# Attention and feed-forward on one core: weighting k's bits, adding x's small term and adding the divisors' small term on ScalarE in place of VectorE

## The chip, the core and the metric

The kernel runs on one core of a Trainium2 chip. The metric is the device time of one execution in microseconds, the median of the runs shown. Five engines work side by side: TensorE (PE, with its weight loads as PEld), VectorE (DVE), ScalarE (ACT), GpSimd (POOL) and SyncE (SP). Each carries out its own list of instructions in order; semaphores make one wait for another. SP, POOL and ACT also issue DMAs.

## The reference

There are 4 batches of 8 heads, 768 positions and 64 dimensions. Attention is allowed only between positions that fall into the same of 64 hash buckets; the result goes through a feed-forward block.

```python
q_bits = (np.einsum('bhsd,dk->bhsk', q, proj) > 0)      # 6 bits each
k_bits = (np.einsum('bhsd,dk->bhsk', k, proj) > 0)
mask = q_bucket[:, :, :, None] == k_bucket[:, :, None, :]
scores = np.where(mask, scale * q @ k.T, -1e9)
attn = exp(scores - max); attn = attn / (attn.sum(-1) + 1e-09)
x = attn @ v                                             # to (3072, 512)
h = x @ w_in                                             # (3072, 2048)
out = (h * erf(softplus(h))) @ w_out
```

## The kernel before

Attention goes over 16 pairs of heads; a pair fills the 128 partitions. For every pair there is a score stage and an av stage.

In the **score stage**, PE makes 12 blocks of scores (score, L557). A block is two bfloat16 matmuls of the bits and four float32 matmuls of q and k, and fills one of three PSUM slots named "big", which are used in turn. The bits are arranged so that two positions of one bucket add nothing to a score and others add a very large negative number; for that k's bits are multiplied by a weight of 2^100 times a small whole number. ACT takes the exponential of every block (exponential, L584) and so frees its slot: block k+3 needs exponential k.

In the **av stage**, PE multiplies the exponentials by v (weigh, L642; 12 matmuls for each half of the keys and each half of the queries). After it, PE makes the signs' inputs of a later pair (bits_of, L845) and the sums of the exponentials, the divisors, of an earlier pair (divisor, L687). Both write one "big" slot, the one before that of block 0 of the next pair. ACT reads that slot twice: sign_of (L854) writes the bits' signs to the tile sg, and keep_divisor (L698) copies the divisors to z. Block 2 needs the slot, and so both of them.

The small tile sg has q's and k's signs. DVE multiplies k's half by the weight (weigh_bits, L864), and POOL sends sg to DRAM (leave_bits, L874) and places it in the tile of the pair's bits (place_bits, L883), from which the next score stage reads.

ACT copies av's two halves to x (leave, L708). No bucket may divide by zero, so every query gets a tiny attention to all keys: the exponentials of the even half have one column more, of ones, so that av's column HS has the sum of v; DVE multiplies it by EPS = 2^-100 to get ev (leave_plain, L714). The divisor gets S x EPS: z goes to DRAM, comes back as 128x12 (spread, gather, on SP), DVE adds S x EPS and takes the reciprocal (invert, L744 and L747), SP sends it out and reads it back widened to r (ungather, widen), DVE makes (x + ev) x r (normalise, L773), and SP sends x to DRAM (send).

Beside this, DVE sums the exponentials (sum_keys, L630) and converts the weights of the feed-forward block from the halves of 64-bit numbers, with two activations on ACT (square_high, L477, and keep_normal, L484; both write a tile "keep"); POOL fetches them. ACT also squares q and k for a bound (measure, L663, tile "junk").

The order on each engine is set by a planner (arrange): each step has an engine, a cost, a rank and the steps that it comes after; the planner plays the stage through with these costs and emits the steps in the order in which they would start, the lowest rank first among those that could start at once. PE's steps form one chain in a fixed order. For instance:

```python
op(weigh_bits, (i,), "DVE", 0.33, (0, n - 6, 1), (("sign_of", i),))
op(keep_divisor, (i,), "ACT", 0.48, (0, 4 * i + 6, -1),
   (("divisor", i), ("spread", i - 2)))
```

The feed-forward block (from 313 us) has a plan of its own: products with w_in (L1248), a gate made by ACT and DVE, products with w_out (L1361). Its first steps also hold the last pair's divisor, invert and normalise.

Of the kernel before, what the change touches and what calls it, by code (L numbers as in the profile page):

```python
# [54 lines left out]
F32 = mybir.dt.float32  # L55
# [3 lines left out]
AF = mybir.ActivationFunctionType  # L59
ALU = mybir.AluOpType  # L60
# [3 lines left out]
P = 128  # L64
# [4 lines left out]
EPS = 2.0**-100  # L69
# [127 lines left out]
def kernel(  # L197
# [11 lines left out]
    nc = tc.nc  # L209
    B, H, S, D = v.shape  # L210
# [5 lines left out]
    HS = S // 2  # L216
# [9 lines left out]
    scale = 1.0 / D**0.5  # L226
    assert D == 64 and S == 768 and DM == JP * P and NT == B * S and NK == 4

    const = ctx.enter_context(tc.tile_pool(name="const", bufs=1))
    dram = ctx.enter_context(tc.tile_pool(name="dram", bufs=2, space=bass.MemoryType.DRAM))  # L230
    misc = ctx.enter_context(tc.tile_pool(name="misc", bufs=1, space=PSUM))
    small = ctx.enter_context(tc.tile_pool(name="small", bufs=3))
# [7 lines left out]
    ones = const.tile([P, D], F32, name="ones")  # L240
    sgn = const.tile([P, 1], F32, name="sgn")
    tiny2 = const.tile([P, 1], F32, name="tiny2")
    cq = const.tile([P, len(GATE_S) + 1], F32, name="cq")
    w_in_sb = const.tile([P, NK, DFF], F32, name="w_in_sb")
    w_out_sb = const.tile([P, NF, DM], F32, name="w_out_sb")
# [51 lines left out]
    nc.vector.tensor_copy(out=weight_q[D + QR : P, :], in_=weight_q[D : D + QR, :])  # L297
    nc.vector.memset(sgn, -(2.0**-27))
    nc.vector.memset(tiny2, TINY * TINY)
    for j, c in enumerate([b for _, b, _ in GATE_S] + [GATE_BIAS]):  # L300
        nc.vector.memset(cq[:, j : j + 1], c)

# [117 lines left out]
    def attention():  # L420
        NS = NPAIR * 4
        with (
# [15 lines left out]
            junk = ep.tile([P, HS], BF16, name="junk")  # L438
            NE = 2 * GC
            e_even = ep.tile([P, NE, 2, HS + 1], F32, name="e_even")  # L440
            nc.vector.memset(e_even[:, :, :, HS : HS + 1], 1.0)
            e_odd = area[:, 0 : NE * S].rearrange("p (n a c) -> p n a c", n=NE, a=2)
            e_last = {}
            pairs = {}
# [250 lines left out]
            def keep_divisor(i):  # L695
                d = pairs[i]
                d["z"] = home(i, "z")
                nc.scalar.copy(out=d["z"], in_=d.pop("z_ps"))  # L698

            def leave(h):  # L700

                i, half = divmod(h, 2)
                d = pairs[i]
                cols = slice(half * HS, (half + 1) * HS)
                if half == 0:
                    d["x"] = home(i, "x")
                x = d["x"][half] if i == NPAIR - 1 else d["x"][:, cols]
                nc.scalar.copy(out=x, in_=d["av", half][:, 0:HS])  # L708

            def leave_plain(i):  # L710

                d = pairs[i]
                d["ev"] = small.tile([P, 1], F32, name="ev", tag="ev")
                nc.vector.tensor_scalar(  # L714
                    out=d["ev"],
                    in0=d["av", 0][:, HS : HS + 1],
                    scalar1=EPS,
                    scalar2=None,
                    op0=ALU.mult,
                )  # L720

            def spread(i):
# [17 lines left out]

            def invert(i):
                d = pairs[i]
                zc = d["zc"]
                nc.vector.tensor_scalar(  # L744
                    out=zc, in0=zc, scalar1=S * EPS, scalar2=None, op0=ALU.add
                )
                nc.vector.reciprocal(out=zc, in_=zc)  # L747

            def ungather(i):
                d = pairs[i]  # L750
# [16 lines left out]
            def normalise(i):  # L767
                d = pairs[i]
                parts = ((d["x"], d["r"]),)
                if i == NPAIR - 1:  # L770
                    parts = ((d["x"][n], d["r"][:, n * HS : (n + 1) * HS]) for n in range(2))
                for x, r in parts:
                    nc.vector.scalar_tensor_tensor(  # L773
                        out=x, in0=x, scalar=d["ev"][:, 0:1], in1=r, op0=ALU.add, op1=ALU.mult
                    )

            def send(i):
                b, j = divmod(i, JP)
# [45 lines left out]
            def op(fn, args, engine, cost, rank, after=(), **more):  # L824
                name = (fn.__name__,) + args
                ops.append(Op(name, engine, cost, rank, lambda: fn(*args), after=after, **more))
# [34 lines left out]

            def weigh_bits(i):

                nc.vector.tensor_scalar(  # L864
                    out=sg[D:P, :],
                    in0=sg[D:P, :],
                    scalar1=weight_q[D:P, 0:1],
                    scalar2=None,
                    op0=ALU.mult,
                )  # L870

            def leave_bits(i):
# [47 lines left out]
            for what, n in order:  # L920
                free = slots[-3] if len(slots) >= 3 else ()
                if what == "score":
                    i = n // 4
                    after = (("double_first",) if i == 1 else ("place_bits", i),)
                    for c in range(GC):
                        free = slots[-3] if len(slots) >= 3 else ()
                        pe(score, (n, c), 0.82 if n or c == 2 else 0.17, after + free)
                        slots.append((("exponential", n, c),))
                elif what == "bits":
                    pe(bits_of, (n,), 0.80 if n > 1 else 1.44, (("start_pair", n),) + free)  # L930
                    slots.append((("sign_of", n),) if n > 1 else (("place_first",),))
                elif what == "divisor":
                    if n != NPAIR - 3:
                        free = ()
                        slots[-1] += (("keep_divisor", n),)
                    else:
                        slots.append((("keep_divisor", n),))
                    pe(divisor, (n,), 0.72, (("sum_keys", n, last_sum(n)),) + free)
                else:
                    h = n // 2  # L940
                    after = (("exponential", n, GC - 1),)
                    if n % 2 == 0:
                        after += (("leave", h - 2), ("leave_plain", (h - 2) // 2))
                    pe(weigh, (n,), 2.0, after)
            sums_after = {}
            for i in range(NPAIR):
# [25 lines left out]
            for i in range(NPAIR - 1):  # L972
                op(
                    keep_divisor,
                    (i,),
                    "ACT",
                    0.48,
                    (0, 4 * i + 6, -1),
                    (("divisor", i), ("spread", i - 2)),
                )  # L980
            for h in range(NH):
                i = h // 2
                op(leave, (h,), "ACT", 0.48, (0, 2 * h, -2), (("weigh", 2 * h + 1), ("send", i - 3)))
                if h % 2 == 0:
                    op(leave_plain, (i,), "DVE", 0.15, (0, 2 * h, 0), (("weigh", 2 * h + 1),))
            for i in range(NPAIR):
                n = 4 * i
                if i:
                    op(
                        start_pair,  # L990
                        (i,),
                        "SP",
                        3.6,
                        (0, n - 6),
                        (("weigh", n - 9), ("bits_of", i - 1))
                        + tuple(("measure", i - 3, m, half) for m in range(2) for half in range(2)),
                        late=3.5,
                    )
                    if i == 1:
                        op(place_first, (), "ACT", 0.9, (0, n - 2, 9), (("bits_of", i),))  # L1000
                        for ab in (1, 0):
                            op(weigh_first, (ab,), "DVE", 0.43, (0, n - 2, 1), (("place_first",),))
                        op(double_first, (), "DVE", 0.35, (0, n - 2, 2), (("weigh_first", 0), ("weigh_first", 1)))
                    else:
                        op(sign_of, (i,), "ACT", 0.6, (0, n - 6, 9), (("bits_of", i), ("leave_bits", i - 1)))
                        op(weigh_bits, (i,), "DVE", 0.33, (0, n - 6, 1), (("sign_of", i),))
                        op(leave_bits, (i,), "POOL", 0.7, (0, n - 6, 2), (("weigh_bits", i),), late=4.0, far=True)
                        op(
                            place_bits,
                            (i,),  # L1010
                            "POOL",
                            1.2,
                            (0, n - 6, 3),
                            (("leave_bits", i), ("score", n - 5, 2), ("clean", i - 2)),
                            late=3.6,
                        )
# [11 lines left out]
                    continue  # L1028
                op(spread, (i,), "SP", 0.4, (0, n, 0), (("keep_divisor", i),), late=3.5, far=True)
                op(gather, (i,), "SP", 0.35, (0, n, 1), (("spread", i),), late=4.5, far=True)  # L1030
                op(invert, (i,), "DVE", 0.4, (0, n + 8, 3), (("gather", i),))
                op(ungather, (i,), "SP", 0.35, (0, n, 2), (("invert", i),), late=3.0, far=True)
                op(
                    widen,
# [4 lines left out]
                    (("ungather", i), ("normalise", i - 2)),  # L1039
                    late=5.0,  # L1040
                )
                op(normalise, (i,), "DVE", 1.02, (0, n + 8, 4), (("widen", i), ("leave", 2 * i + 1)))
                op(send, (i,), "SP", 0.35, (0, n, 4), (("normalise", i),), late=2.2)
            for n in range(2):
                op(clean, (n,), "POOL", 1.4, (0, 4 * n), (("score", 4 * n + 3, 2),), late=0.3)
# [787 lines left out]
```

## Time and profile before

| what | value |
|---|---|
| runs shown | 904.62, 904.65, 905.37 us; median 904.65 |
| the profiled execution | 904.72 us, its span 902.9 us |
| granted TensorE clock | 0.998 |
| attention | from the start to 313 us |
| PE busy in 20 to 320 us | all of it, but for 0.02 us |
| DVE busy in 145 to 170 us | 23.78 of 25 us |
| ACT busy in 145 to 170 us | 21.23 of 25 us |
| first exponential of a pair (143.49 us) | 0.82 us |
| one activation of measure, and the next start after it | 0.52 us, 0.51 us |

The profile is one execution taken by the hardware profiler. A row of a group gives line, engine, operation, the tiles written and read, shapes and count, then the busy time in us and the mean of one in ns, then the engine's idle time ahead of them and what ended it. In a timeline, instructions of one kind that follow each other are merged; the second number is the length of the merged row. An engine's neighbouring instructions overlap a little, so the distance of two starts can be less than the first one's length. The ends of matmuls are modelled, so a short wait of PE need not be seen as idle time; it is seen in the distance of starts.

### The profile page before, as it was taken

What the parts mean: (1) busy time and instruction counts of PE and PEld (TensorE: products, weight loads), DVE (VectorE), ACT (ScalarE), POOL (GpSimd) and SP (SyncE); (2) the same over time, 40 slices, a digit from 0 to 9 for tenths busy, and PEclk for the clock granted to TensorE, in tenths of its full rate; (3) what the DMA queues carried; (4) which work ended last, traced back from release to release, by engine and by line L of the source; (5) the groups of instructions that cost most, each with busy time, mean ns of one, the idle gap of its engine ahead of it and who ended that gap; (6) DMA issues with size and microseconds to landing.
All of it is one profiled execution on the core that took longest, in us unless ns stands there. A gap on an engine that the chain in (4) does not pass through costs nothing.

```text
span 902.9 us, 12780 instructions
## 1 busy us (share of the span) xinstructions
PE 894.3 (99%) x5016; PEld 670.9 (74%) x5016; DVE 668.5 (74%) x837; ACT 563.3 (62%) x808; POOL 57.9 (6%) x95
## 2 busy tenths in 40 slices
PE   9999999999999999999999999999999999999997
PEld 5455554455544588888888888888888888888886
DVE  5999999999999879995666556666776666655652
ACT  6788888788886668855645455545655555545520
POOL 1211211111110000000000001000100010000000
PEclk9999999999999999999999999999999999999999
DMA  9547655667551322202231013211421122111211
GB/s 228 149 128 183 200 166 142 196 173 195 154 157 60 101 89 65 82 36 70 59 106 58 14 49 103 82 36 47 105 83 36 36 74 78 35 36 57 63 68 50
DMA packets 65156, 86.82 MB, mean 96 GB/s; under 512 B 34364, under 2 KB 47772, under 8 KB 65088
## 3 DMA queue, kind: packets, MB, share of 16 engines
q1 hardware_dynamic: 56528, 63.81, 24.8%
q0 software_dynamic: 8112, 21.66, 8.6%
q8 instruction: 41, 0.67, 0.3%
q10 hardware_dynamic: 448, 0.46, 0.2%
q14 instruction: 27, 0.22, 0.1%
HBM read 64.67 MB, written 17.30 MB: 91 GB/s over the span
## 4 chain that ended last, share of the span: by engine, by line
PE 99%; DVE 0%; issue 0%; ACT 0%; DVEq 0%
PE M L1361 32%; PE X L1248 29%; PE st L557 17%; PE av L642 14%; PE M L1248 3%; PE bits L845 1%; PE bits L687 1%; PE warm L807 0%; PE bits L377 0%; PE z_ps L687 0%; DVE e L1288 0%; DVE h L1270 0%; ACT both L390 0%; DVE u L1396 0%; DVE norms L1754 0%
## 5 line engine op out<-in xcount | busy, mean ns | idle before, releaser
L1288 DVE SCALAR_TENSOR_TENSOR e<-w,e 128x1024 f32<-128x1024 f32 x144 | 173.7, 1220 | 8.4 <-ACT w L1282 3.9
L1248 PE MATMUL X<-area,w_in_sb 128*128 128x256 f32 x680 | 160.6, 379 | 0.0
L1282 ACT ACTIVATE w<-h,cq 128x1024 f32<-128x1024 f32 x144 | 155.6, 1136 | 0.1
L557 PE MATMUL st<-q,k 64*128 64x384 f32 x768 | 155.1, 482 | 0.0
L1270 DVE TENSOR_TENSOR h<-X,h 128x512 f32<-128x512 f32 x65 | 44.8, 689 | 144.4 <-PE X L1248 144.4
L1248 PEld LDWEIGHTS X<-area,w_in_sb 128*128 128x128 f32 x680 | 129.2, 190 | 17.6
L1361 PE MATMUL M<-w_out_sb,h 128*128 128x256 f32 x576 | 141.1, 379 | 0.0
L1248 PE MATMUL X<-area 128*128 128x256 f32 x520 | 122.8, 379 | 0.0
L1361 PEld LDWEIGHTS M<-w_out_sb,h 128*128 128x128 f32 x576 | 109.4, 190 | 14.9
L1266 ACT COPY h<-X 128x512 f32<-128x512 f32 x85 | 49.3, 580 | 111.4 <-PE X L1248 111.3
L1248 PEld LDWEIGHTS X<-area 128*128 128x128 f32 x520 | 98.8, 190 | 13.4
L1278 ACT ACTIVATE e<-h,cq 128x1024 f32<-128x1024 f32 x48 | 55.1, 1148 | 85.9 <-DVE h L1270 85.8
L1361 PE MATMUL M<-wt,S 128*128 128x256 f32 x384 | 95.1, 379 | 0.0
L557 PEld LDWEIGHTS st<-q,k 64*128 64x128 f32 x768 | 68.8, 187 | 29.7 <-issue 27.2
L630 DVE TENSOR_TENSOR area<-area 128x1536 f32<-128x1536 f32 (+1 forms) x46 | 79.2, 1723 | 7.5 <-ACT area L584 6.3
L1361 PEld LDWEIGHTS M<-wt,S 128*128 128x128 f32 x384 | 73.0, 190 | 9.9
L584 ACT ACTIVATE e_even<-st 128x768 f32<-128x768 f32 x96 | 70.6, 822 | 0.4 <-PE st L557 0.3
L584 ACT ACTIVATE area<-st 128x768 f32<-128x768 f32 x90 | 68.0, 817 | 0.0
L642 PE MATMUL av<-e_even,v 128*64 128x385 f32 x384 | 65.6, 490 | 0.0
L557 PE MATMUL st<-both 64*128 64x384 bf16 x384 | 63.5, 323 | 0.3 <-ACT both L390 0.3
L1303 DVE TENSOR_TENSOR h<-h,e 128x1024 f32<-128x1024 f32 x48 | 57.9, 1220 | 4.6 <-ACT e L1299 4.6
L642 PE MATMUL av<-area,v 128*64 128x384 f32 x360 | 60.6, 486 | 0.0
(129 smaller groups left out, 976.8 us busy)
## 6 DMA issues: line engine op xcount, KB each, us to landing
wt<-wt SPq DMA_DIRECT2D x24, 768.0 KB, 4.2
raw<-in_w_out_dram POOLq DMA_DIRECT2D x16, 512.0 KB, 4.2
raw<-in_w_in_dram POOLq DMA_DIRECT2D x14, 512.0 KB, 4.6
v<-in_v_dram SPq DMA_DIRECT2D x32, 192.0 KB, 4.6
q<-in_qkT_dram SPq DMA_DIRECT2D x30, 192.0 KB, 4.2
k<-in_qkT_dram SPq DMA_DIRECT2D x30, 192.0 KB, 4.7
r<-rd SPq DMA_DIRECT2D x30, 192.0 KB, 3.7
xs<-x SPq DMA_DIRECT2D x15, 384.0 KB, 3.0
```

Source lines behind the costliest of these rows:

```text
L557: nc.tensor.matmul(out=st[:, ab, 0:HS], lhsT=d["k" + src][rows, keys], rhs=d["q" + src][rows, cols], start=(part == 0), stop=(part == 1),)
L584: nc.scalar.activation(out=e[:, :, 0:HS], in_=st[:, :, 0:HS], func=AF.Exp, scale=scale)
L630: nc.vector.tensor_tensor(out=into, in0=one, in1=two, op=ALU.add)
L642: nc.tensor.matmul(out=d["av", half][rows, 0:w], lhsT=d["v"][:, g * GC + c, rows], rhs=e[:, ab, 0:w], start=(g == 0 and c == 0), stop=(g = ...
L1248: nc.tensor.matmul(out=d[where][:, u, :], lhsT=a[:, kc, f : f + P], rhs=b[:, kc, :], start=(first and u == 0 and kc == 0), stop=(last and ...
L1266: nc.scalar.copy(out=quarter(p, q), in_=st[p][where])
L1270: nc.vector.tensor_tensor(out=h, in0=st[p][where], in1=h, op=ALU.add)
L1278: nc.scalar.activation(out=s, in_=unit(p, v), func=AF.Sigmoid, bias=cq[:, n : n + 1])
L1282: nc.scalar.activation(out=q, in_=unit(p, v), func=AF.Sigmoid, scale=GATE_S[j][0], bias=cq[:, j : j + 1])
L1288: nc.vector.scalar_tensor_tensor(out=s, in0=st[p].pop(("q", v, j)), scalar=GATE_S[j][2], in1=s, op0=ALU.add, op1=ALU.mult,)
L1303: nc.vector.tensor_tensor(out=h, in0=h, in1=st[p].pop(("s", v)), op=ALU.mult)
L1361: nc.tensor.matmul(out=banks[name][:, sub, :], lhsT=a[:, u, sub * P : (sub + 1) * P], rhs=b[:, u, :], start=(c == 0 and k == 0), stop=(c = ...
```

## The change

Three small computations go from DVE to ACT, each into an activation with a per-partition operand where that can be.

- k's weight: the DVE multiply becomes an activation Copy whose scale is the weight's column (64x384, in place in sg).
- ev: the extra column holds EPS in place of ones, so av's column HS is ev itself; ACT copies it (128x1), and both copies of av to x become activations Identity with ev as the bias. normalise is a plain multiply by r.
- the divisors' S x EPS: the copy of z becomes an activation Identity with a column "least" as the bias; invert is the reciprocal alone.

The planner's costs and ranks are changed to match, and so the order that it emits.

```diff
+    least = const.tile([P, 1], F32, name="least")
...
+    nc.vector.memset(least, S * EPS)
...
-            nc.vector.memset(e_even[:, :, :, HS : HS + 1], 1.0)
+            nc.vector.memset(e_even[:, :, :, HS : HS + 1], EPS)
...
                 d["z"] = home(i, "z")
-                nc.scalar.copy(out=d["z"], in_=d.pop("z_ps"))
+                nc.scalar.activation(
+                    out=d["z"], in_=d.pop("z_ps"), func=AF.Identity, bias=least[:, 0:1]
+                )
...
-                nc.scalar.copy(out=x, in_=d["av", half][:, 0:HS])
-
-            def leave_plain(i):
-
-                d = pairs[i]
-                d["ev"] = small.tile([P, 1], F32, name="ev", tag="ev")
-                nc.vector.tensor_scalar(
-                    out=d["ev"],
-                    in0=d["av", 0][:, HS : HS + 1],
-                    scalar1=EPS,
-                    scalar2=None,
-                    op0=ALU.mult,
+                if half == 0:
+                    d["ev"] = small.tile([P, 1], F32, name="ev", tag="ev")
+                    nc.scalar.copy(out=d["ev"], in_=d["av", 0][:, HS : HS + 1])
+                nc.scalar.activation(
+                    out=x, in_=d["av", half][:, 0:HS], func=AF.Identity, bias=d["ev"][:, 0:1]
                 )
...
-                zc = d["zc"]
-                nc.vector.tensor_scalar(
-                    out=zc, in0=zc, scalar1=S * EPS, scalar2=None, op0=ALU.add
-                )
-                nc.vector.reciprocal(out=zc, in_=zc)
+                nc.vector.reciprocal(out=d["zc"], in_=d["zc"])
...
-                    nc.vector.scalar_tensor_tensor(
-                        out=x, in0=x, scalar=d["ev"][:, 0:1], in1=r, op0=ALU.add, op1=ALU.mult
-                    )
+                    nc.vector.tensor_tensor(out=x, in0=x, in1=r, op=ALU.mult)
...
-                nc.vector.tensor_scalar(
-                    out=sg[D:P, :],
-                    in0=sg[D:P, :],
-                    scalar1=weight_q[D:P, 0:1],
-                    scalar2=None,
-                    op0=ALU.mult,
+                nc.scalar.activation(
+                    out=sg[D:P, :], in_=sg[D:P, :], func=AF.Copy, scale=weight_q[D:P, 0:1]
                 )
...
-                        after += (("leave", h - 2), ("leave_plain", (h - 2) // 2))
+                        after += (("leave", h - 2),)
...
                     keep_divisor,
                     (i,),
                     "ACT",
-                    0.48,
+                    0.58,
...
-                op(leave, (h,), "ACT", 0.48, (0, 2 * h, -2), (("weigh", 2 * h + 1), ("send", i - 3)))
-                if h % 2 == 0:
-                    op(leave_plain, (i,), "DVE", 0.15, (0, 2 * h, 0), (("weigh", 2 * h + 1),))
+                op(leave, (h,), "ACT", 0.58 if h % 2 else 0.78, (0, 2 * h, -2), (("weigh", 2 * h + 1), ("send", i - 3)))
...
-                        op(weigh_bits, (i,), "DVE", 0.33, (0, n - 6, 1), (("sign_of", i),))
+                        op(weigh_bits, (i,), "ACT", 0.5, (0, n - 6, 10), (("sign_of", i),))
...
-                op(invert, (i,), "DVE", 0.4, (0, n + 8, 3), (("gather", i),))
+                op(invert, (i,), "DVE", 0.23, (0, n + 8, 3), (("gather", i),))
...
-                op(normalise, (i,), "DVE", 1.02, (0, n + 8, 4), (("widen", i), ("leave", 2 * i + 1)))
+                op(normalise, (i,), "DVE", 0.93, (0, n + 8, 4), (("widen", i), ("leave", 2 * i + 1)))
```

## The prediction, as it was put on record

> **What bounds the kernel now.** I read the page's busy times first, then who TensorE (PE) waited for, then the groups of instructions by form over the first 440 us, then the timelines of ScalarE (ACT) and PE beside each other. The page:
>
> ```profile
> PE 894.3 (99%) x5016; PEld 670.9 (74%) x5016; DVE 668.5 (74%) x837; ACT 563.3 (62%) x808; POOL 57.9 (6%) x95
> ```
>
> PE is busy in 99% of the span, and the chain that ended last is PE for 99% of it. A microsecond counts only if PE's stream is held or let go. All of PE's recorded waits are these:
>
> ```profile
> PE warm L807 <- DVE ones L253: 1.0, 1, 1.0
> PE M L1248 <- DVE h L1270: 0.7, 1, 0.7
> PE st L557 <- ACT both L390: 0.3, 1, 0.3
> ```
>
> So VectorE (DVE), though 24 of 25 us busy in most stretches of attention, holds PE in one place only, 0.7 us at 338.22 us, after attention. But this view hides small holds, because the modelled end of a matmul fills them. They show in the chain in order of time, as the distance from one pair's score stage to the next: 19.13 us in most pairs, but 19.42 from 103.93, 19.30 from 180.79 and 19.17 three times: 0.58 us lost in all. What a held pair looks like on ACT, then on PE (start us, length us, engine, line, tiles):
>
> ```profile
> 104.00 0.58 ACT L854 ACTIVATE sg<-bits,sgn 128x384 bf16<-128x384 f32 x1 [0.98 <-PE bits L687]
> 104.48 0.67 ACT L477 ACTIVATE keep<-raw 128x512 f32<-128x512 f32 x1
> 105.03 0.48 ACT L698 COPY z<-bits 128x384 f32<-128x384 f32 x1
> 105.39 2.24 ACT L584 ACTIVATE e_even<-st 128x768 f32<-128x768 f32 x3
> 107.48 0.76 ACT L484 ACTIVATE keep<-keep,tiny 128x512 int32<-128x512 f32 x1
> 108.09 2.25 ACT L584 ACTIVATE e_even<-st 128x768 f32<-128x768 f32 x3
> ```
>
> ```profile
> 104.68 0.33 PE L557 MATMUL st<-both 64*128 64x384 bf16 x2
> 104.84 0.81 PE L557 MATMUL st<-q,k 64*128 64x384 f32 x4
> 105.57 0.34 PE L557 MATMUL st<-both 64*128 64x384 bf16 x2
> ...
> 108.15 0.82 PE L557 MATMUL st<-q,k 64*128 64x384 f32 x4
> 108.99 0.34 PE L557 MATMUL st<-both 64*128 64x384 bf16 x2
> ```
>
> A score block costs PE 0.807 us. Block 2 was due at 105.49 and began at 105.57, 0.05 us after z's end (105.03 + 0.48): the three PSUM slots make block 2 wait for the sign and for z, which read the slot before block 0. In the same way block k+3 waits for exponential k: block 6 began at 108.99, just after the exponential that stood behind the keep (108.09 + 0.84), 0.18 late. That is the place where this change can act: **the first microseconds of each score stage on ACT**.
>
> **The skill.** "ScalarE: Activation LUTs", section "What ACT_TABLE_LOAD costs", says that every per-partition pointer operand (bias or scale) adds about 93 ns to an activation, and that neighbours overlap by about 93 ns. The trace agrees: sign, with a bias pointer, 581 ns beside 472 to 480 for copies of the same size, and z starts 0.48 after sign. Its section "Rules for kernel authors" gives plain adds and multiplies to VectorE; the rows below bear that out here (320 ns on DVE). The forecast takes the trace's durations.
>
> ```profile
> L484 ACT ACTIVATE keep<-keep,tiny 128x512 int32<-128x512 f32 x32 | 23.2, 724 | 0.7
> L773 DVE SCALAR_TENSOR_TENSOR x<-x,ev,r 128x768 f32<-128x768 f32 x15 | 15.1, 1011 | 0.0
> L708 ACT COPY x<-av 128x384 f32<-128x384 f32 x30 | 14.4, 480 | 41.7 <-PE av L642 41.1 <-DVE ev L714 0.5
> L854 ACT ACTIVATE sg<-bits,sgn 128x384 bf16<-128x384 f32 x14 | 8.1, 581 | 11.8 <-PE bits L687 11.5 <-PE bits L845 0.3
> L698 ACT COPY z<-bits 128x384 f32<-128x384 f32 x13 | 6.1, 472 | 0.0
> L864 DVE TENSOR_SCALAR sg<-sg,weight_q 64x384 bf16<-64x384 bf16 x14 | 4.5, 320 | 0.6
> L744 DVE TENSOR_SCALAR zc<-zc 128x12 f32<-128x12 f32 x16 | 2.6, 162 | 0.0
> L714 DVE TENSOR_SCALAR ev<-av 128x1 f32<-128x1 f32 x16 | 2.4, 149 | 0.5 <-ACT x_last L708 0.3 <-ACT x L708 0.2
> ```
>
> **The change part by part.** PE's instruction order is the same in both built programs; DVE's, ACT's, and in a few places POOL's and SP's, are re-planned.
>
> *DVE loses* 16 x 0.149 (ev) + 14 x 0.320 (weigh) + 16 x 0.162 (divisor's add) = 9.5 us, and normalise falls from 1.01 to about 0.96 (the 128x768 sum rows, 958 ns), 0.8 us more. On the path: nothing, since no PE wait in attention ends on DVE. The hold at 338.22 stays: before it DVE idles 0.88 us for PE's bound matmul, so the 0.16 us saved ahead of that only lengthens the idling. The new memset (least) falls into DVE's 3.2 us wait for proj_in at the start.
>
> *ACT gains in the av stage:* one ev copy (128x1; between 0.20, the accumulator read of that size, and 0.48, a whole L708 copy; I take 0.2), 0.03 for the x that waits for it, and 0.1 on each of two x by the pointer rule: 0.43 us a pair. Cover: ACT idles there 0.66, 2.04 and 0.98 us (before the two x and the sign, 156 to 162 us). If it were gone, sign and block 2 would be late. Cost 0. av's PSUM is written again only in the next pair.
>
> *ACT gains at the head of the score stage:* weigh, and z grown by 0.1 to 0.58. Weigh (64x384, from SBUF, scale pointer) has no row. Nearest: L484, pointer, 512 wide, 724 ns; less 128 x 0.83 ns (a 768-wide sign, 0.90, against the 384-wide, 0.58) gives 0.62; sign itself 0.58; below, the Square of this size without a pointer, 0.52. I take 0.60, next start 0.50 later. It waits for sign's write: L484 starts 0.03 after L477's end.
>
> Time from block 0: sign starts at 0.14, ends 0.72; blocks 2, 3, 5 and 6 are due at 1.62, 2.43, 4.05 and 4.86. Before, z ended at 1.09 and the first exponential at 1.85, both with over 0.4 to spare. The new instruction list has two orders:
>
> - Sign, weigh, z (5 pairs). Weigh 0.75 to 1.35, z 1.25 to 1.83, block 2 at 1.88: **0.26 late**. Exponentials start at 1.73 and 2.42 (0.69 apart when ACT is behind); in 4 pairs the plan puts one squaring (measure, 0.51) next, so the third starts at 3.62, ends 4.45, and block 5, now due at 1.88 + 3 x 0.807 = 4.30, begins at 4.50: 0.20 late. In the fifth the measure comes one later: exponential 3 starts at 4.31, ends 5.15; block 6, due at 5.11, begins at 5.20: 0.09. Sum 4 x 0.46 + 0.35 = 2.2 us.
> - Sign, z, weigh (8 pairs). z ends at 1.20, in time. Weigh 1.09 to 1.69, first exponential 1.59 to 2.43, block 3 at 2.48: 0.05 late. A pair of the old trace with a keep in that place (exponential 1.60 after block 0) lost 0.04 in its period; I take 0.04: 0.3 us. Later exponentials regain 0.12 each, so measures or keeps put after the sixth or later cost nothing.
> - One pair has no z: the exponential starts at 1.24, free.
>
> Sum 2.5 us, less the 0.58 of old holds (all in pairs that get the new order) = 1.9; about 0.01 more per held pair (period against counted holds: 0.29 against 0.28), 0.1. **Net +2.0 us.** It is against the profiled execution, 904.72 (span 902.9), which lies 0.07 from the median 904.65: 906.7.
>
> *Queues.* Behind weigh stand the exponentials, as costed. POOL's store of the bits leaves 0.4 to 0.8 us later, with the weight fetch queued behind it; the bits are placed at 147.64 for use at 161.59, the fetch (144.39) is read at 154.31: covered. SP's spread leaves up to 0.8 later; from its issue at 143.57 the gather was issued at 147.30, and the reciprocal came at 155.43, so with a second landing as long over 4 us are spare. The few swaps among SP's and POOL's DMAs fall inside such margins: 0.
>
> **Rivals.**
> 1. *The holds are smaller.* With weigh at its lower end, 0.52, z in the first order starts 0.08 earlier, the first hold is 0.17, and the second order has none: 4 x 0.37 + 0.26 = 1.7, less 0.58 = +1.1: 905.8, which is no change within 0.2%. It decides from weigh under about 0.57. For it: the Square row. Against it: the pointer's 0.1 in sign.
> 2. *DVE's relief is what counts*, ACT absorbing its additions: the 0.58 us of holds and the 0.7 at 338.22 go: 903.4 at best, no measurable gain. For it: DVE at 24 of 25 us. Against it: both large holds stand after ACT's z and exponential, not after DVE.
> 3. *ACT falls behind for good.* If weigh or its wait costs 0.2 us more, the second order holds block 3 by 0.25 (8 x 0.2 = 1.6 more) and the first by 5 x 0.2 = 1.0 more: +4.6, 909.3. For it: scale pointers and chained waits have few rows. Against it: L484's 0.03.
>
> **How the numbers follow.** Forecast 0.53 (906.2 to 908.0), rival 1 0.31, rival 2 0.04, rival 3 0.12. A measurement of this kernel tells about 0.2% (1.8 us) from no change, so the forecast lies just outside that bound, and I leave a tenth of its cases within it: slower 0.60, same 0.38, faster 0.02. The range takes in rival 1's value and part of rival 3's: 905.3 to 908.4.
>
> **What would show it.** PE's score-to-score periods near 19.6 in the five pairs with weigh ahead of z, near 19.17 in the eight others; z ending about 1.83 after block 0 in the five; weigh near 0.60; the stretch from 345 us on unchanged in length; DVE busy about 10 us less, ACT about 17 more. I am wrong if weigh is much shorter, if PE's block 2 doesn't wait for z, or if a hold appears in the av stage.

## The result, and the profile after

The changed kernel takes **910.73 us** (median of 909.55 to 911.01), the kernel before 904.85 beside it: a ratio of 1.0064, interval 1.0054 to 1.0074. It is slower, as forecast, but by 5.9 us in place of 2.0, and outside the range. Its profiled execution is 910.92 us, with a span of 908.8.

The page's busy times moved between the engines as forecast: DVE has 9.3 us less, ACT 17.4 more, and PE, whose work is the same, 3.6 more.

```profile
PE 897.9 (99%) x5016; PEld 672.7 (74%) x5016; DVE 659.2 (73%) x792; ACT 580.7 (64%) x838; POOL 58.1 (6%) x95
```

All of PE's recorded waits, as shown for the kernel before:

```profile
PE st L559 <- ACT z L700: 1.1, 5, 0.2
PE warm L798 <- DVE ones L254: 1.0, 1, 1.0
PE M L1233 <- DVE h L1255: 0.7, 1, 0.7
PE st L559 <- ACT both L392: 0.3, 1, 0.3
```

The first row is new: block 2 waits for z in five pairs, 0.2 us each. The 0.7 us that PE waits after attention stayed. Nothing else appears, though more than this was lost; again the small holds are hidden by the modelled ends of matmuls.

The lengths of the new instructions were forecast well. ACT's groups by form, over the first 440 us (busy us, mean ns):

```profile
L855 ACT ACTIVATE sg<-sg,weight_q 64x384 bf16<-64x384 bf16 x14 | 8.5, 610 | 0.4
L845 ACT ACTIVATE sg<-bits,sgn 128x384 bf16<-128x384 f32 x14 | 8.1, 580 | 8.0 <-PE bits L689 7.8 <-PE bits L836 0.2
L700 ACT ACTIVATE z<-bits,least 128x384 f32<-128x384 f32 x13 | 7.5, 576 | 0.1
```

Weigh takes 0.61 us (forecast 0.60), z 0.58 (0.58). So the lengths don't explain the miss.

**Where the time went.** From block 1 of the first pair's score stage to block 1 of the last pair's the kernel before takes 288.18 us, the changed one 293.26: **+5.08**. I call this stretch "attention" below. From there to the end, 606.3 became 606.5. The stretch began 0.62 later (at 9.02 for 8.40 us); in the profiled runs of all kernels below it begins anywhere from 8.08 to 9.18, with the change and without, so this is not counted as the change's. The last 0.3 us of the profiled difference lie outside the span.

The distance from one pair's score stage to the next was 19.13 in most pairs before. Now it is 19.72 in four of the five pairs with weigh ahead of z and 19.61 in the fifth (forecast near 19.6); 19.42 to 19.43 in four of the eight pairs with z ahead of weigh and 19.52 to 19.53 in the other four (forecast 19.17); 19.25 in the pair without z (forecast 19.13). A pair with z ahead of weigh, on ACT (start us, length us, engine, line, tiles):

```profile
67.06 0.58 ACT L845 ACTIVATE sg<-bits,sgn 128x384 bf16<-128x384 f32 x1 [0.87 <-PE bits L689]
67.54 0.57 ACT L700 ACTIVATE z<-bits,least 128x384 f32<-128x384 f32 x1
68.14 0.61 ACT L855 ACTIVATE sg<-sg,weight_q 64x384 bf16<-64x384 bf16 x1
68.77 4.33 ACT L586 ACTIVATE e_even<-st 128x768 f32<-128x768 f32 x6
73.08 0.81 ACT L586 ACTIVATE area<-st 128x768 f32<-128x768 f32 x1
73.91 0.72 ACT L486 ACTIVATE keep<-keep,tiny 128x512 int32<-128x512 f32 x1
```

Read the starts against the ends. z starts 0.10 before sign's end, as neighbours do in this trace where neither needs the other's result. (Where one does, it starts 0.03 after the other's end, as the prediction took for weigh behind sign.) Weigh starts at 68.14, 0.025 us **after** z's end (68.11), and the first exponential 0.024 **after** weigh's end (68.75). Then six exponentials take 4.33 us, 0.72 for each, overlapped again; but the first activation of another kind, the keep at 73.91, again starts 0.025 after the end of the one before. Each of these three places costs about 0.12. On PE in the same pair:

```profile
67.74 0.33 PE L559 MATMUL st<-both 64*128 64x384 bf16 x2
...
68.55 0.33 PE L559 MATMUL st<-both 64*128 64x384 bf16 x2
...
69.64 0.34 PE L559 MATMUL st<-both 64*128 64x384 bf16 x2
```

Blocks start 0.81 apart, but block 3, due at 69.36, starts at 69.64, after the first exponential: 0.28 late. A pair with weigh ahead of z, on ACT, then on PE (blocks 1 and 2):

```profile
47.34 0.58 ACT L845 ACTIVATE sg<-bits,sgn 128x384 bf16<-128x384 f32 x1 [0.87 <-PE bits L689]
47.96 0.61 ACT L855 ACTIVATE sg<-sg,weight_q 64x384 bf16<-64x384 bf16 x1
48.59 0.58 ACT L700 ACTIVATE z<-bits,least 128x384 f32<-128x384 f32 x1
49.07 1.50 ACT L586 ACTIVATE e_even<-st 128x768 f32<-128x768 f32 x2
```

```profile
48.03 0.33 PE L559 MATMUL st<-both 64*128 64x384 bf16 x2
...
49.22 0.34 PE L559 MATMUL st<-both 64*128 64x384 bf16 x2 [0.23 <-ACT z L700]
```

z starts 0.025 after weigh's end, not 0.10 before it. Block 0 of this pair began at 47.21; z's end, 49.17, lies 1.96 after it, where 1.83 was forecast, and block 2 is 0.39 late in place of 0.26. So the question for the experiments was not how long weigh is but **why it doesn't overlap its neighbours**: because of its function, its pointer, its type, its writing in place, its number of partitions, or the order it stands in.

### The profile page after: what moved, and what is told of

Its sections match the earlier page's. It is cut to its first block, busy times and chain, and to the rows that moved or that the text cites. A ratio compares the mean times of both kernels' runs of the same rounds, so it can differ in the third digit from the quotient of the medians.

```text
span 908.8 us, 12773 instructions
## 1 busy us (share of the span) xinstructions
PE 897.9 (99%) x5016; PEld 672.7 (74%) x5016; DVE 659.2 (73%) x792; ACT 580.7 (64%) x838; POOL 58.1 (6%) x95
## 4 chain that ended last, share of the span: by engine, by line
PE 95%; ACT 3%; DVE 0%; issue 0%; DVEq 0%
PE M L1346 32%; PE X L1233 29%; PE st L559 14%; PE av L644 14%; PE M L1233 3%; PE bits L836 1%; PE bits L689 1%; ACT sg L845 1%; ACT sg L855 1%; ACT z L700 1%; ACT e_even L586 1%; PE warm L798 0%; PE bits L379 0%; PE z_ps L689 0%; DVE e L1273 0%
```

## The experiments

"Ratio" is to the kernel before on the same chip; where there is none, the kernel had one execution, and the reading rests on its trace.

**Is it weigh, or one of the other two moves?** Everything of the change, but weigh back on VectorE with its old cost and rank:

```diff
-                nc.scalar.activation(
-                    out=sg[D:P, :], in_=sg[D:P, :], func=AF.Copy, scale=weight_q[D:P, 0:1]
+                nc.vector.tensor_scalar(
+                    out=sg[D:P, :], in0=sg[D:P, :], scalar1=weight_q[D:P, 0:1], ...
...
-    op(weigh_bits, (i,), "ACT", 0.5, (0, n - 6, 10), (("sign_of", i),))
+    op(weigh_bits, (i,), "DVE", 0.33, (0, n - 6, 1), (("sign_of", i),))
```

> The change with weigh_bits back on VectorE (its old cost and rank); ev, the biased copies of x and the biased z stay on ScalarE. Theory (the weigh instruction alone makes the time, by the holds at the head of each score stage): about the time before, 904.9 +- 0.6, score-to-score periods 19.13 to 19.45 as before, no hold of block 3. Rival (the longer z and the ev and x copies matter too, or the re-planned order does): 906 to 908, with holds left in most pairs.

Measured: 904.84 us, ratio 1.0004 (0.9995 to 1.0013); attention 288.27. The moves of x's and the divisors' small terms are not told from no change. As far as the time can tell, weigh is the whole cost.

The other half: the kernel before with weigh alone on ScalarE (the same instruction and plan entry; z a plain copy).

> The kernel before with weigh_bits alone put on ScalarE (the change's cost and rank); z stays a plain copy, ev and the divisor's add stay on VectorE. Theory: most of the 5.9 us, 908.8 to 910.0, periods of about 19.6 where weigh stands ahead of z and about 19.4 where it stands after it. Rival (it takes the biased z too): under 907.

Measured: 912.07 us, ratio 1.0084 (1.0067 to 1.0101); attention 295.20, +7.0. Weigh alone costs more than the whole change: with other costs around it the plan puts weigh ahead of z in seven pairs, with a squaring right after the first exponential, and these last 19.87 to 19.94 us. The size was missed; what one instruction costs hangs on what the planner sets behind it. One of the seven pairs on ACT, from z on; weigh ended at 48.24:

```profile
48.26 0.48 ACT L698 COPY z<-bits 128x384 f32<-128x384 f32 x1
48.63 0.82 ACT L584 ACTIVATE e_even<-st 128x768 f32<-128x768 f32 x1
49.48 0.52 ACT L663 ACTIVATE junk<-q 128x384 bf16<-128x384 f32 x1
```

The exponential overlaps z by 0.10, but the squaring starts 0.024 after the exponential's end (0.023 to 0.026 in all seven). In the change, where z is an activation with a bias, the squaring behind "weigh, z, exponentials" overlaps by 0.12 or more in all five pairs. So part of the higher price is one stop more in each of these pairs.

**The instruction, or the order that the planner makes of it?** The change's own order on every engine, with only the weigh instruction emitted on VectorE (its planned place kept):

> The change with its plan kept (weigh_bits is still planned on ScalarE at a cost of 0.5, so all instructions are emitted in the change's order), but the weigh instruction itself goes to VectorE. Theory (the instruction on ScalarE makes the holds): none of block 2 and 3, periods 19.13 to 19.25, 904.9. Rival (the change's plan, with squarings right after the second exponential, costs by itself): some holds of block 5 or later stay, 906 to 907.

Measured: 904.19 us, ratio 0.9999 (0.9990 to 1.0007); attention 287.61, all pairs 19.13. The order is innocent; the instruction on ACT is the cost.

The other way, z ahead of weigh in all pairs:

```diff
-    op(weigh_bits, (i,), "ACT", 0.5, (0, n - 6, 10), (("sign_of", i),))
+    op(weigh_bits, (i,), "ACT", 0.5, (0, n - 6, 10), (("sign_of", i), ("keep_divisor", i - 3)))
```

> The change with one more dependency in the plan: weigh_bits comes after keep_divisor of the same slot, so that the order is sign, z, weigh in all pairs. Theory (ahead of z, weigh holds block 2 by 0.39 us and block 5 by 0.19; after z it holds block 3 by 0.28): the five pairs fall from 19.6-19.7 to about 19.4, 1.2 us less than the change, 909.5. Rival (ScalarE's total work sets it, the order moves the hold only): no different from the change, 910.7.

Measured: 910.00 us, ratio 1.0060 (1.0043 to 1.0076); attention 293.59, no shorter than the change's: the rival's answer. In four of the five pairs block 2 is in time now, but block 3 is 0.28 late, and a squaring, planned after the fourth exponential, makes block 7 another 0.22 late: they last 19.64 for 19.72. The fifth got a keep between sign and z, and lasts 20.03 (block 2 is 0.22 late, block 3 another 0.66); one of the eight got the squaring too, and lasts 19.64 for 19.43. The holds were pushed to other blocks.

**Its function?** Weigh as Identity instead of Copy, the pointer kept:

```diff
-                    out=sg[D:P, :], in_=sg[D:P, :], func=AF.Copy, scale=weight_q[D:P, 0:1]
+                    out=sg[D:P, :], in_=sg[D:P, :], func=AF.Identity, scale=weight_q[D:P, 0:1]
```

> The change with weigh as an Identity activation in place of a Copy, with the same scale pointer; the plan is the same. In the change the instruction after weigh starts 0.025 us after weigh's end, where other neighbours overlap by 0.10. If the function Copy is what keeps them apart, they overlap again here, and the holds shrink by about 0.1 (the order weigh, z) to 0.25 (the order z, weigh), some 2 us in all: about 908.5. If the scale pointer, the bfloat16 input or the half of the partitions does it, nothing moves: 910.7.

Measured: 910.55 us; attention 293.29; the gaps are still +0.024 to +0.026. Not the function.

**Its pointer?** A constant scale of 2.0 (the bits' weights are left out):

```diff
-                    out=sg[D:P, :], in_=sg[D:P, :], func=AF.Copy, scale=weight_q[D:P, 0:1]
+                    out=sg[D:P, :], in_=sg[D:P, :], func=AF.Copy, scale=2.0
```

> The change with a constant scale (2.0) in weigh in place of the pointer to the weight's column: the weights of the bits are left out. Plan, shape, bfloat16 and half of the partitions as in the change. If the scale pointer keeps weigh apart from its neighbours, they overlap again by about 0.10, weigh takes about 0.51, and the holds fall to about 0.1 (weigh, z: block 2) and 0 (z, weigh: block 3), the time to about 906. If bfloat16 or the half of the partitions does it, the gaps of 0.025 stay: about 910.

Measured: 908.12 us; attention 292.07. ACT in a pair with z ahead:

```profile
66.45 0.57 ACT L700 ACTIVATE z<-bits,least 128x384 f32<-128x384 f32 x1
67.05 0.52 ACT L855 ACTIVATE sg<-sg 64x384 bf16<-64x384 bf16 x1
67.60 0.81 ACT L586 ACTIVATE e_even<-st 128x768 f32<-128x768 f32 x1
```

Weigh is 0.09 shorter, and still stands alone: it starts 0.025 after z's end (67.02), and the exponential 0.024 after its end. So the pointer costs its 0.09 us, 1.2 us of attention in all, but not the overlap. (The rest of the shorter time lies outside attention: the stretch begins 0.9 earlier, at 8.08, and what follows it takes 605.8.) From the other side, the kernel before with a pointer of ones as the scale in square_high, on all partitions:

```diff
-                nc.scalar.activation(out=sq, in_=high.bitcast(F32), func=AF.Square)
+                nc.scalar.activation(out=sq, in_=high.bitcast(F32), func=AF.Square, scale=ones[:, 0:1])
```

> The kernel before with a scale pointer (a column of ones) in square_high, a float32 activation of all 128 partitions, 32 in all; weigh is on VectorE. If a scale pointer keeps an activation apart from its neighbours, square_high now starts 0.025 after its predecessor's end, its successor likewise, and it takes 0.1 longer; the two pairs with a square between sign and z are held some 0.3 us more, and the time is 905.3 to 906. If the pointer isn't the cause, it overlaps its neighbours by 0.1 as before: 904.8.

Measured: 904.93 us; attention 288.51. The squares grow from 688 to 780 ns, and still overlap by about 0.10 those neighbours that don't need their result.

**Its type?** The kernel before with measure reading bfloat16 zeros (the norms' bound is left out):

```diff
-                    in_=pairs[i]["qk"[n]][:, cols],
+                    in_=junk,
```

> The kernel before with the squarings of measure reading the bfloat16 tile junk (zeros, all 128 partitions) in place of q and k; the bound on the norms is left out. If a bfloat16 input is what keeps an activation apart, measure now starts 0.025 after the exponential ahead of it has ended, and the exponential after it 0.025 after its end, where both overlapped by 0.1 before; the time is 905.5 to 908, as measures stand among the exponentials. If not, it overlaps as before: 904.8.

Measured: 906.12 us, with a late begin (9.18); attention 288.21, as before. The overlaps stay at 0.10 to 0.15. Not the type; and as junk is here both read and written, not the writing in place.

**Its partitions?** Weigh works on the 64 partitions of k's bits. The change with weigh over all 128, q's rows weighted by 1:

```diff
+    nc.vector.memset(weight_q[0:D, :], 1.0)
...
-                    out=sg[D:P, :], in_=sg[D:P, :], func=AF.Copy, scale=weight_q[D:P, 0:1]
+                    out=sg, in_=sg, func=AF.Copy, scale=weight_q[:, 0:1]
```

> The change with weigh over all 128 partitions (q's half with weights of 1), still bfloat16 and in place. If the half of the partitions keeps weigh apart from its neighbours, they overlap by 0.10 now and the time falls to about 907; if the bfloat16 input (or the in-place write) does it, gaps of 0.025 and holds stay as in the change: 910 to 911.

Measured: 906.01 us (905.62 for one execution of the kernel before beside it); attention 289.97, +1.79. The pair shown first for the change (lines are one higher here):

```profile
66.37 0.58 ACT L846 ACTIVATE sg<-bits,sgn 128x384 bf16<-128x384 f32 x1 [0.87 <-PE bits L690]
66.85 0.57 ACT L701 ACTIVATE z<-bits,least 128x384 f32<-128x384 f32 x1
67.31 0.62 ACT L856 ACTIVATE sg<-sg,weight_q 128x384 bf16<-128x384 bf16 x1
67.82 2.91 ACT L587 ACTIVATE e_even<-st 128x768 f32<-128x768 f32 x4
```

Twice the rows, the same length (0.616 us), and now weigh starts 0.11 before z's end and the exponential 0.11 before weigh's. The holds of the blocks are nearly those that the prediction gave for the change: 0.26 and 0.19 in the four pairs, 0.26 and 0.08 in the fifth, and by the periods 0.02 to 0.03 in the eight; and the later holds of 0.10 are gone.

And the reverse: the kernel before with measure on the upper 64 partitions (half of the norms left out), nothing else changed:

```diff
+            nc.vector.memset(stats, 0.0)
...
-                    out=junk,
-                    in_=pairs[i]["qk"[n]][:, cols],
+                    out=junk[D:P, :],
+                    in_=pairs[i]["qk"[n]][D:P, cols],
...
-                    accum_out=stats[:, n, i, half : half + 1],
+                    accum_out=stats[D:P, n, i, half : half + 1],
```

> The kernel before with the squarings of measure over partitions 64 to 127 alone, float32 (the norms of each pair's first head are left out). If an activation on half of the partitions is kept apart from its neighbours, the gaps around measure become 0.025; if not, they stay at -0.1 and the time at 904.8.

Measured: 907.66 us; attention 290.83, +2.65: less work, more time.

```profile
66.62 0.81 ACT L585 ACTIVATE e_even<-st 128x768 f32<-128x768 f32 x1
67.46 0.52 ACT L664 ACTIVATE junk<-q 64x384 bf16<-64x384 f32 x1
67.89 0.18 ACT L664 ACTIVATION_READ_ACCUMULATOR junk<-q 64x1 f32 x1
68.10 3.62 ACT L585 ACTIVATE e_even<-st 128x768 f32<-128x768 f32 x5
```

The squaring starts 0.024 after the exponential's end (all 38 such neighbours in attention: 0.023 to 0.026; before, 0.10 to 0.15 ahead of it), and the exponential 0.024 after the accumulator read (23 of 23). But between the squaring and its accumulator read, both on the same 64 partitions, the overlap of 0.09 stays, in 64 of 64. (A squaring right behind an accumulator read starts 0.03 after it, 18 of 18, but so it does in the kernel before.) So it is the **change between 128 and 64 partitions**, either way, that ends the overlap. Most pairs now last 19.40: blocks 4 and 11 are 0.13 late each.

**Is there a version without the loss?** On GpSimd instead, with sign_of planned after the divisor:

```diff
-                nc.scalar.activation(
-                    out=sg[D:P, :], in_=sg[D:P, :], func=AF.Copy, scale=weight_q[D:P, 0:1]
+                nc.gpsimd.tensor_scalar(
+                    out=sg[D:P, :], in0=sg[D:P, :], scalar1=weight_q[D:P, 0:1], ...
...
-    op(sign_of, (i,), "ACT", 0.6, (0, n - 6, 9), (("bits_of", i), ("leave_bits", i - 1)))
-    op(weigh_bits, (i,), "ACT", 0.5, (0, n - 6, 10), (("sign_of", i),))
+    op(sign_of, (i,), "ACT", 0.6, (0, n - 6, 9), (("bits_of", i), ("leave_bits", i - 1), ("divisor", i - 3)))
+    op(weigh_bits, (i,), "POOL", 0.6, (0, n - 6, 1), (("sign_of", i),))
```

> The change with weigh_bits on GpSimd, ahead of the store that it issues anyway, and sign_of planned after the divisor, so that no weight conversion stands between sign and z. Theory (only the head of the score stage on ScalarE counts): no hold of blocks 2 and 3, all periods 19.13 to 19.2, 0.5 us under the kernel before at best, 904.2. Rival (the weighing or the store on GpSimd comes too late for the next score stage, or VectorE's place matters): holds of block 0, 906 or more.

Measured: 904.03 us, ratio 0.9995 (0.9986 to 1.0003); attention 287.61, all pairs 19.13. Weigh takes about 1.57 us there (GpSimd's spans are rough in this profile); only GpSimd's own store of the bits waits for it, and PE's recorded waits are the three of the kernel before. The trace has 0.6 us of holds fewer than before; the time can't tell it from no change.

And on ScalarE with both repairs, all 128 partitions and z ahead of weigh (the two edits above together):

> The change with the weighing run over all 128 partitions (the rows of k weighted by 1) and planned behind z of its own pair, so that z stands ahead of it in all pairs. Theory (half of the partitions is what drains ScalarE): weighing and neighbours overlap by 0.10 us, block 3 is held by at most 0.05 us in the z-first pairs; the place that the squaring is re-planned to may hold one later block by 0.1 in the five former pairs, so attention grows by 0 to 0.6 us against the kernel before: 904.4 to 905.8. Rival (the order of z and weighing matters more than the overlap): attention stays about 3 us longer or more, 907 or over.

Measured: 905.09 us, ratio 1.0006 (0.9998 to 1.0015); attention 288.87, +0.69, a little over what was expected. Of the pairs with z, seven last 19.15 to 19.16, five 19.22 to 19.23 (the squaring after the fourth exponential; 0.08 in block 7, where it cost 0.22 with half the partitions), and one 19.76, where a keep is planned ahead of z. So ScalarE can do the work at a price that the time can't tell from none, but there is nothing to be gained from it either.

## Why the prediction was wrong

Right, by its own steps:

- **Where it acts.** All of the loss in attention lies in the first microseconds of each score stage and in what follows from them; PE waits for z and for the first exponential, as it said. After attention nothing changed (606.3 and 606.5).
- **What costs nothing.** DVE's relief, ACT's additions in the av stage, the divisor's path and the queues: with weigh on DVE or its planned place kept, no difference can be measured (1.0004 and 0.9999).
- **The lengths.** Weigh 0.61 for 0.60, z 0.58, ACT 17.4 more for about 17, DVE 9.3 less for about 10. Weigh started 0.03 after sign's end, as taken.
- **The two orders** and which block each holds.

Wrong: **"next start 0.50 later"**, the distance from weigh's start to the next one's. It gave the steps "Weigh 0.75 to 1.35, z 1.25 to 1.83" and "Weigh 1.09 to 1.69, first exponential 1.59 to 2.43". It took the overlap of 0.1 us from instructions on 128 partitions, and weigh has 64. Measured, the next start is 0.633 to 0.635 later, and behind z weigh starts 0.60 after z's start, not the 0.48 taken. The terms of the sum:

| term | forecast | measured | difference |
|---|---|---|---|
| five pairs, weigh ahead of z: block 2 late | 0.26 | 0.39 | 5 x 0.13 = 0.65 |
| eight pairs, z ahead of weigh: block 3 late | 0.04 | 0.28 | 8 x 0.24 = 1.92 |
| later blocks, behind the first activation of another kind (four of the eight) | 0 | 0.10 to 0.12 | 0.42 |
| the pair without z | 0 | 0.11 | 0.11 |

These make 3.1 us, and 2.0 + 3.1 is the 5.1 measured. The second term is where the price of one assumption doubled: z's side and weigh's far side both lie ahead of the first exponential, and the forecast had used up all the slack, so that each 0.12 counted in full. With the overlap given back (all 128 partitions) attention grew by 1.79, the forecast's 2.0 within 0.2; so the rest of its working held.

"Measures or keeps put after the sixth or later cost nothing" failed too, in three pairs of the third term; in its fourth pair a squaring stands after the fifth exponential, and in the pair without z a square_high after the fourth. All have one reason: the first activation of another kind after weigh's run of exponentials starts 0.025 after the end of the one before it, in all nine pairs in which exponentials follow weigh, and in none with 128 partitions.

Rival 3 came nearest, with 909.3 and block 3 held by 0.25. It supposed 0.2 us more in weigh or in its wait for sign; the price was of that size, but it lay between weigh and its neighbours. It was given 0.12: "against it" stood only a wait, and the statement of the Trainium skill ("ScalarE: Activation LUTs", "What ACT_TABLE_LOAD costs") on the overlap was taken as true of every activation. On 128 partitions the traces agree with it where neither activation needs the other's result (0.10), and with the 93 ns of a pointer (0.52 to 0.61 in weigh, 0.69 to 0.78 in square_high); across a change to 64 partitions the measurement decides: no overlap.

Left open: what the chip does between two such instructions, and why the first activation of another kind behind the exponentials is stopped as well when all of its neighbours have 128 partitions. No run was made for this, but the traces narrow it. With z between weigh and the exponentials the second stop is there when z is a plain copy (7 of 7, weigh alone on ScalarE) and absent when z is an activation with a bias (5 of 5 in the change, and again in the runs with Identity and with the constant scale). So exponentials behind weigh are not enough to bring it; whether z's operation or its bias lifts it isn't shown. Whether a change to fewer than 64 partitions, or to the lower 64, costs the same wasn't tried.

## What to carry to other kernels

Cost a moved instruction by the distance between starts that it makes on both its sides, not by its length; where no row of the trace has its shape, partitions included, the overlap is an unknown with two ends, and the sum has to carry both. On ScalarE, work on half the partitions among work on all of them was dearer here than the same work on all: fill the other rows with a harmless operand, if they may be written. And when holds of a tenth of a microsecond are in question, read the distances between the score stages, since PE's recorded waits showed 1.1 us of a loss of 5.1.

## What the runs showed of the hardware

- ScalarE's neighbours on 128 partitions overlapped by about 0.10 us or more where neither waited for the other or for PE; so did a squaring and its accumulator read on the same 64 (0.09). Between 128 and the upper 64 the second started 0.023 to 0.026 us after the first one's end, both ways (0.012 to 0.013 in three of the squarings on 64): some 0.12 us per change of partitions. Where the second needs the first one's result, it started 0.03 after its end with or without such a change (sign and weigh, 64 or 128 partitions), so there the change costs nothing more.
- The stop came back once later: with exponentials right behind the 64-partition weigh, the next activation of another kind, five to nine places on, also started 0.025 after its neighbour's end, in nine of nine pairs of the change (14 of 14 with z ahead of weigh in all pairs).
- Weigh took 0.61 us on 64 partitions and 0.62 on 128; half the rows saved nothing.
